# K and V transposed on PE as 4-byte pairs in a one-token attention kernel with its backward pass

## The chip, the cores and the metric

The kernel runs on one core of one Trainium2 chip. The metric is the device time of one execution in microseconds (us), as a median over several executions. Before the change it is 417.73 us (417.38 to 418.01, 4 runs). Ratios in this text are computed as the mean time of one kernel's fast runs over the mean time of the other kernel's fast runs of the same rounds, so they are not quite the ratio of the medians quoted beside them.

PE is the matrix engine (PEld its weight loads), DVE the vector engine, ACT the scalar engine, POOL and SP the two engines that here mostly issue transfers. A "DMA engine" is one of the 16 that move the core's data.

## The reference

One query token attends to a cache of 4096 keys and values in 32 heads of 128, in bf16; a small MLP is mixed in by a sigmoid gate. The kernel must return the output and the gradients of nine inputs, among them those of the whole K and V cache.

```python
q = (x @ wq)                                   # x: 1x640, wq: 640x4096 -> 32 heads of 128
s = einsum("bhqd,bhkd->bhqk", q, k_cache) * 128 ** -0.5
p = softmax(s)
o = einsum("bhqk,bhkd->bhqd", p, v_cache)
out = g * (o @ wo) + (1 - g) * mlp(x)          # g = sigmoid(sum(x * gate_w))
# and the vector-Jacobian product of out with grad_out for all inputs but B_x
# ... k_cache, v_cache and their gradients: 32 x 4096 x 128 bf16, 33.5 MB each
```

The four large tensors are 134 of the 165 MB that are moved.

## The kernel before

A K or V tile holds one head: 128 partitions, and on each partition 32 rows of 128 bf16 numbers (J = 32 blocks, 8 KB per partition). The products with the query (for K) and with the incoming gradient (for V) contract over the 128 numbers of a row, so each block is transposed on PE first, copied from PSUM to SBUF by ACT, and used as the stationary operand of a small matmul:

```python
def transposes(src, c):                       # chunk c of 4: eight blocks
    tp = tr_ps.tile([P, 8, P], BF16, name="tr", tag="tr")
    for t in range(8):
        nc.tensor.transpose(tp[:, t, :], src[:, c * 8 + t, :], ident_bf[:])
    sb = tsb.tile([P, 8, P], BF16, name="tT", tag="tT")
    nc.scalar.copy(f32v(sb[...]), f32v(tp[...]))          # shapes cut
    return sb

def products(out, tb, c, vec):
    for t in range(8):
        j = c * 8 + t
        nc.tensor.matmul(out[:, j:j + W], lhsT=tb[:, t, :], rhs=vec.to_broadcast([P, W]), start=True, stop=True)
```

Two more sums run over the same tiles without a transpose:

```python
def o_part(a, b):                              # o = sum over j of V_j^T e_j
    for j in range(a, b):
        nc.tensor.matmul(O, lhsT=vts[h][:, j, :], rhs=st["e"][:, j:j + 1].to_broadcast([P, W]), ...)
...
for j in range(J):                             # dq
    nc.tensor.matmul(DQ, lhsT=kts[h][:, j, :], rhs=ds[:, j, 0:1].to_broadcast([P, W]), ...)
```

The loads of K and V are issued by SP three heads ahead, into four buffers each. The gradients dK and dV are outer products on DVE, stored by POOL:

```python
def load_k(h):
    kts[h] = kv_in.tile([P, J, Dh], BF16, name="Kn", tag="Kn", bufs=KB)
    nc.sync.dma_start(kts[h][:], Kv[h])
...
nc.gpsimd.dma_start(dVv[h], st["dV"][:])
```

Every matmul here is two PE instructions, a weight load and the matmul. The program is fully unrolled: 13,864 of these on PE alone.

## Time and profile before

| what | value | view |
|---|---|---|
| time | 417.73 us (span of the profiled run 415.7) | runs |
| traffic | 165.06 MB, 397 GB/s over the span | queue table |
| DMA share from 5 to 374 us | 1.01 at 415 GB/s | busy time by stretch |
| PE, DVE busy from 5 to 374 us | 295 and 284 of 369 us | busy time by stretch |
| PE instructions | 6,932 weight loads, 6,932 matmuls | page, part 1 |

The first lines are the busy time by stretch of the kernel before: for each stretch the busy us and the number of instructions of the five engines, the clock granted to PE, the mean busy share of the 16 DMA engines, and what they moved.

```profile
core 0: us, PE busy (x) PEld busy (x) DVE busy (x) ACT busy (x) POOL busy (x), PEclk, DMA share, GB/s
5.00:374.00 369.00, 295.24 (x6715) 272.23 (x6716) 284.36 (x740) 168.88 (x382) 41.17 (x73) 0.95 1.01 415
374.00:403.00 29.00, 10.40 (x217) 8.90 (x216) 22.99 (x60) 4.21 (x11) 7.32 (x11) 0.69 0.95 379
403.00:416.00 13.00, 0.00 (x0) 0.00 (x0) 0.00 (x0) 0.00 (x0) 0.00 (x0) 0.50 0.06 23
```

To the eye the DMA is full until 403 us. Here is the same view of the last microseconds in 5 us steps:

```profile
395.00:400.00 5.00, 0.45 (x1) 0.18 (x1) 4.75 (x20) 0.00 (x0) 1.45 (x2) 0.50 1.01 394
400.00:405.00 5.00, 0.27 (x1) 0.09 (x1) 0.88 (x5) 0.25 (x1) 0.00 (x0) 0.50 0.66 251
405.00:410.00 5.00, 0.00 (x0) 0.00 (x0) 0.00 (x0) 0.00 (x0) 0.00 (x0) 0.50 0.06 26
```

From 405 to 410 us no engine computes and the DMA share is 0.06, one sixteenth, at 26 GB/s. One DMA engine is at work; the other 15 have finished.

The queue table of the page (queue, kind: packets, MB, share of the 16 engines' time) lists the loads (q1), the stores (q0) and the fetching of instructions (q8, q14):

```profile
q1 hardware_dynamic: 14116, 82.03, 48.6%
q0 software_dynamic: 12112, 82.03, 47.7%
q8 instruction: 54, 0.88, 0.8%
q14 instruction: 14, 0.11, 0.1%
```

These are the groups of instructions that the change touches (line, engine, operation, out<-in, shapes, count | busy us, mean ns of one | idle before and what ended it). L537 is the PSUM copy, L535 the transposes, L543 the products, L385 the only matmuls whose weights are read with a stride (36 bytes):

```profile
L537 ACT COPY tT<-tr 128x512 f32<-128x512 f32 x256 | 142.9, 587 | 153.1 <-PE tr L535 153.0
L543 PEld LDWEIGHTS <-tT 128*128 128x128 bf16 x2048 | 75.8, 98 | 37.0 <-ACT tT L537 31.6
L535 PE MATMUL tr<-ident_bf,Kn 128*128 128x128 bf16 x1024 | 79.2, 230 | 9.4 <-DMA Kn<-in_A_k_cache_dram 8.2
...
L535 PEld LDWEIGHTS <-Kn 128*128 128x128 bf16 x1024 | 66.2, 104 | 10.9 <-DMA Kn<-in_A_k_cache_dram 9.3
...
L543 PE MATMUL sA<-qdc,tT 128*128 128x48 bf16 x1024 | 49.2, 188 | 23.0 <-ACT dq_all L659 16.3
...
L385 PEld LDWEIGHTS <-w_sb 128*96 128x96 bf16 x90 | 17.6, 272 | 1.6 <-issue 0.6
```

Last, three lines of PE's timeline (start us, duration us, engine, line, operation). Eight bf16 transposes take 0.61 us, of which the last is 0.22, so they start 56 ns apart; the fp32 transpose of L609 occupies PE for 0.11 us before the next one starts:

```profile
201.13 1.05 PE L535 MATMUL tr<-ident_bf,Vn 128*128 128x128 bf16 x16
202.03 0.28 PE L609 MATMUL sA<-ident_f,m 128*128 128x128 f32 x1
202.14 0.61 PE L535 MATMUL tr<-ident_bf,Vn 128*128 128x128 bf16 x8
```

### The profile page before, as it was taken

The numbers are of one execution on the slowest core, as the hardware profiler recorded it, in microseconds if no ns is written. First come the engines' busy times: TensorE is split into PE (matmuls) and PEld (weight loads), VectorE is DVE, ScalarE is ACT, GpSimd is POOL, SyncE is SP. The second block draws the span as 40 slices with busy tenths as digits, with TensorE's granted clock in tenths as the row PEclk, the third lists the DMA queues.
The fourth block names the chain that finished last, engine by engine and source line by source line (L and its number), as shares of the span: only waits on it lengthen the run. The fifth ranks groups of instructions, "written<-read, shape, count | busy, mean of one in ns | idle before, by whom it ended". The sixth has DMA issues, their size and how long they took to land.

```text
span 415.7 us, 15639 instructions
## 1 busy us (share of the span) xinstructions
PE 305.6 (74%) x6932; PEld 281.1 (68%) x6932; DVE 308.2 (74%) x804; ACT 174.4 (42%) x394; POOL 49.3 (12%) x92
## 2 busy tenths in 40 slices
PE   0787999888998788788877688429888788876200
PEld 0676888888987677787767687428777678876200
DVE  2348666665679999989897688528999997967850
ACT  1354444334445455354533346305553545553000
POOL 0001110111110111121111112001111111132310
PEclk9999999969999999989996899958999999998655
DMA  8999999999999999999999999999999999998980
GB/s 280 419 401 335 420 424 417 420 423 423 421 423 420 420 404 415 424 420 423 423 410 426 423 414 411 419 422 381 405 411 423 419 419 422 421 422 351 401 314 14
DMA packets 26336, 165.06 MB, mean 397 GB/s; under 512 B 2812, under 2 KB 2812, under 8 KB 10012
## 3 DMA queue, kind: packets, MB, share of 16 engines
q1 hardware_dynamic: 14116, 82.03, 48.6%
q0 software_dynamic: 12112, 82.03, 47.7%
q8 instruction: 54, 0.88, 0.8%
q14 instruction: 14, 0.11, 0.1%
q10 hardware_dynamic: 40, 0.01, 0.0%
HBM read 82.03 MB, written 82.03 MB: 395 GB/s over the span
## 4 chain that ended last, share of the span: by engine, by line
DMA 37%; DVE 30%; PE 21%; ACT 6%; issue 2%; ACTq 0%; DVEq 0%
DMA Kn<-in_A_k_cache_dram 30%; PE tr L535 7%; DVE dK_sb L557 7%; DVE dV_sb L557 6%; DMA out_dram<-dK_sb 6%; ACT tT L537 5%; DVE junk L354 4%; PE sA L601 3%; PE sA L543 3%; PE sB L654 3%; DVE junk L268 3%; PE h_ps L385 2%; DVE junk L486 2%; DMA vec_rows<-in_gate_w_dram 1%; DVE wo_g L343 1%
## 5 line engine op out<-in xcount | busy, mean ns | idle before, releaser
L537 ACT COPY tT<-tr 128x512 f32<-128x512 f32 x256 | 142.9, 587 | 153.1 <-PE tr L535 153.0
L543 PEld LDWEIGHTS <-tT 128*128 128x128 bf16 x2048 | 75.8, 98 | 37.0 <-ACT tT L537 31.6
L535 PE MATMUL tr<-ident_bf,Kn 128*128 128x128 bf16 x1024 | 79.2, 230 | 9.4 <-DMA Kn<-in_A_k_cache_dram 8.2
L557 DVE TENSOR_TENSOR dV_sb<-p_bf,qd 128x2048 bf16<-128x2048 bf16 x64 | 78.0, 1218 | 4.1 <-DMA out_dram<-dK_sb 4.1
L557 DVE TENSOR_TENSOR dK_sb<-ds_bf,qd 128x2048 bf16<-128x2048 bf16 x64 | 77.7, 1216 | 0.0
L535 PEld LDWEIGHTS <-Kn 128*128 128x128 bf16 x1024 | 66.2, 104 | 10.9 <-DMA Kn<-in_A_k_cache_dram 9.3
L535 PE MATMUL tr<-ident_bf,Vn 128*128 128x128 bf16 x1024 | 72.8, 221 | 0.2 <-DMA Vn<-in_A_v_cache_dram 0.2
L543 PE MATMUL sA<-qdc,tT 128*128 128x48 bf16 x1024 | 49.2, 188 | 23.0 <-ACT dq_all L659 16.3
L535 PEld LDWEIGHTS <-Vn 128*128 128x128 bf16 x1024 | 63.2, 100 | 1.4 <-issue 0.7
L543 PE MATMUL sB<-qdc,tT 128*128 128x48 bf16 x1024 | 46.3, 183 | 0.6 <-issue 0.6
L654 PE MATMUL sB<-ds_bf,Kn 128*128 128x48 bf16 x1024 | 32.6, 185 | 7.7 <-DVE ds_bf L643 4.8
L584 POOL DMA_DIRECT2D out_dram<-dV_sb x32 | 18.3, 571 | 169.1 <-DVE dV_sb L557 82.1
L601 PEld LDWEIGHTS <-Vn 128*128 128x128 bf16 x1024 | 30.3, 96 | 10.4 <-issue 10.3
L601 PE MATMUL sA<-e_bf,Vn 128*128 128x48 bf16 x1024 | 30.9, 183 | 7.4 <-DVE zs L621 5.4
L574 POOL DMA_DIRECT2D out_dram<-dK_sb x31 | 17.7, 570 | 153.1 <-DVE rz L623 84.6
L654 PEld LDWEIGHTS <-Kn 128*128 128x128 bf16 x1024 | 29.7, 97 | 8.3 <-issue 8.3
L605 DVE TENSOR_REDUCE m<-sA 128x1 f32<-128x32 f32 x32 | 6.1, 189 | 31.7 <-PE sA L543 31.5
L268 DVE SCALAR_TENSOR_TENSOR junk<-wo_g,da_bc 128x640 bf16<-128x640 bf16 x32 | 26.3, 821 | 2.9 <-DMA wo_g<-in_A_wo_dram 1.2
L354 DVE SCALAR_TENSOR_TENSOR junk<-wq_g,dq_bc 128x1024 bf16<-128x1024 bf16 (+1 forms) x25 | 25.1, 1004 | 0.2
L385 PE MATMUL h_ps<-cols_bf,w_sb 128*96 128x1 bf16 x90 | 18.3, 314 | 1.2 <-ACT qd L279 0.5
L641 DVE TENSOR_SCALAR_CACHE_REDUCE dj<-sB,rz 128x128 f32<-128x128 f32 x32 | 11.1, 345 | 10.8 <-PE sB L635 10.8
L385 PEld LDWEIGHTS <-w_sb 128*96 128x96 bf16 x90 | 17.6, 272 | 1.6 <-issue 0.6
(137 smaller groups left out, 277.5 us busy)
## 6 DMA issues: line engine op xcount, KB each, us to landing
Kn<-in_A_k_cache_dram SPq DMA_DIRECT2D x32, 1024.0 KB, 27.0
Vn<-in_A_v_cache_dram SPq DMA_DIRECT2D x32, 1024.0 KB, 27.8
out_dram<-dV_sb POOLq DMA_DIRECT2D x32, 1024.0 KB, 12.3
out_dram<-dK_sb POOLq DMA_DIRECT2D x31, 1024.0 KB, 12.4
wq_g<-in_A_wq_dram SPq DMA_DIRECT2D x4, 1280.0 KB, 21.8
wo_g<-in_A_wo_dram SPq DMA_DIRECT2D x8, 640.0 KB, 13.3
out_dram<-wo_g POOLq DMA_DIRECT2D x8, 640.0 KB, 11.3
out_dram<-dwq_t POOLq DMA_DIRECT2D x5, 896.0 KB, 16.2
```

What stands on the lines that cost most here:

```text
L268: nc.vector.scalar_tensor_tensor(junk[:, 0:D], in0=wos[g][:, i, :], scalar=1.0, in1=da_bc[:], op0=ALU.mult, op1=ALU.mult, accum_out=gp["do ...
L354: nc.vector.scalar_tensor_tensor(junk[:, c0:c1], in0=wqs[w][:, rc, c0:c1], scalar=1.0, in1=dq_bc[:, w * WG * Dh + c0:w * WG * Dh + c1], op ...
L385: nc.tensor.matmul(hps[a][:, fc:fc + 1], lhsT=w1_sb[:, rc, :].rearrange("p (q c) -> p q c", c=FCN)[:, :, fc], rhs=x_bf[:, rc:rc + 1], star ...
L535: nc.tensor.transpose(tp[:, t, :], src[:, c * 8 + t, :], ident_bf[:])
L537: nc.scalar.copy(f32v(sb[:].rearrange("p a b -> p (a b)")), f32v(tp[:].rearrange("p a b -> p (a b)")))
L543: nc.tensor.matmul(out[:, j:j + W], lhsT=tb[:, t, :], rhs=vec.to_broadcast([P, W]), start=True, stop=True)
L557: nc.vector.tensor_tensor(dst[:, a:b, :].rearrange("p j (a b) -> p j a b", b=2), col[:, a:b, :].unsqueeze(2).to_broadcast([P, n, Dh // 2, 2]),
L574: nc.gpsimd.dma_start(dKv[h], st["dK"][:])
L584: nc.gpsimd.dma_start(dVv[h], st["dV"][:])
L601: nc.tensor.matmul(O, lhsT=vts[h][:, j, :], rhs=st["e"][:, j:j + 1].to_broadcast([P, W]), start=(j == 0), stop=(j == J - 1))
L641: nc.vector.tensor_scalar(dj[:], PT, rz[:], None, ALU.mult, ALU.add, accum_out=dd[:])
L654: nc.tensor.matmul(DQ, lhsT=kts[h][:, j, :], rhs=ds[:, j, 0:1].to_broadcast([P, W]), start=(j == 0), stop=(j == J - 1))
```

## The change

Two neighbouring bf16 numbers are moved through the transpose as one 4-byte number. One transpose then handles two blocks: 16 per K or V tile, 32 per head, in place of 64. After it, partition p holds a pair of numbers (2p', 2p'+1) of the even block (p < 64) or the odd block. The query is therefore laid out as two columns per half of the pair, zero in the other block's partitions ("block-diagonal"), and two accumulating matmuls, one per half of the pair, give the products of both blocks. The number of products stays at 64 per head. The intent was to halve the transposes.

```diff
     def transposes(src, c):
-        tp = tr_ps.tile([P, 8, P], BF16, name="tr", tag="tr")
-        for t in range(8):
-            nc.tensor.transpose(tp[:, t, :], src[:, c * 8 + t, :], ident_bf[:])
-        sb = tsb.tile([P, 8, P], BF16, name="tT", tag="tT")
...
+        tp = tr_ps.tile([P, 4, P], F32, name="tr", tag="tr")
+        flat = f32v(src[:].rearrange("p j d -> p (j d)"))
+        for t in range(4):
+            k = c * 4 + t
+            nc.tensor.transpose(tp[:, t, :], flat[:, k * P:(k + 1) * P], ident_f[:])
+        sb = tsb.tile([P, 4, P], F32, name="tT", tag="tT")
+        nc.scalar.copy(sb[...], tp[...])
+        return sb[...].bitcast(BF16).rearrange("p (a b two) -> p a two b", a=4, two=2)
 
     def products(out, tb, c, vec):
-        for t in range(8):
-            j = c * 8 + t
-            nc.tensor.matmul(out[:, j:j + W], lhsT=tb[:, t, :], rhs=vec.to_broadcast([P, W]), start=True, stop=True)
+        for t in range(4):
+            k = c * 4 + t
+            for par in range(2):
+                nc.tensor.matmul(out[:, 2 * k:2 * k + W], lhsT=tb[:, t, par, :],
+                                 rhs=vec[:, par, :].unsqueeze(1).to_broadcast([P, W // 2, 2]),
+                                 start=(par == 0), stop=(par == 1))
# cut: the masks mask2 and sel2, three zeroed tiles for the columns, and per group of four heads
# two small DVE products, one matmul and two ACT copies that build the block-diagonal columns,
# in place of two small DVE products
```

## The prediction

> What bounds the kernel now: the DMA. In the table of busy time by stretch, the DMA engines' share is 1.01 from 5 to 374 us at 415 GB/s, with PE busy 295 of those 369 us and DVE 284. From 374 to 403 us it is still 0.95 (one hole, 0.71 from 375 to 380). The 165.06 MB (queue table) at the 420 GB/s of the good slices alone take about 393 us of the 415.7 us span. The Trainium skill ("DMA: Bandwidth & Descriptors", "Where 436 GB/s comes from") gives 435 GB/s as the fabric's ceiling; these slices are near it. The change moves no data byte. K loads wait for buffers that PE frees, but stores keep the DMA full meanwhile.
>
> What the change does, per head (K and V):
> - Transposes: 64 bf16 become 32 fp32. In the timeline eight bf16 transposes take 0.61 us, the last one 0.22: 56 ns start to start. The fp32 transposes already in the kernel (lines 609, 635) last 292 and 319 ns against about 220, and the next transpose follows line 609's after 0.11 us (202.03 to 202.14). So I take 111 ns, two bf16 transposes: 64 x 56 = 3.58 us become 32 x 111 = 3.55 us. Nothing is saved. The skill ("TensorE: Matmul & The Clock Gate", "Weight-path perf modes") says fast weight load has no win for fp32; the fp32 loads here do take 138 to 164 ns against 98, but I expect them hidden behind the matmuls.
> - PSUM copies on ACT: the same 8, 128x512 fp32, 587 ns.
> - Products: the same 64 matmuls of 48 columns (25 ns start to start), but their weights are read with a step of 2 elements. The only strided weights here (line 385, step 18) load in 272 ns instead of 98, 179 ns apart. I expect step 2 to be nearly free; at worst about 60 ns (estimate: 179 ns for 96 columns is 1.9 ns each, every one on a new 16-byte line; here 32 lines). That adds 64 x 35 ns = 2.2 us.
> - Preparation, 8 groups: two small DVE operations stay two; a matmul and two short ACT operations are added, about 0.8 us of latency.
> - 2,048 fewer PE instructions: the instruction queue's 0.88 MB falls by some 0.13 MB, 0.3 us of DMA.
>
> How much is on the critical path: almost nothing. The chain of waits shows PE transposes at 7%, between DMA waits (37%), and their sum doesn't change. A head takes 11.6 us on average and 9.1 us where it catches up, so even 2 us more on PE would mostly be hidden. The tail after 374 us is stores, DVE (23 of 29 us) and the last landings.
>
> Predicted: 417.4 us, 415 to 422 in 8 of 10. Faster by over 2%: 0.02; within 2%: 0.90; slower by over 2%: 0.08.
>
> What would show it: DMA share about 1.0 from 5 to 374 us; 1,024 transposes at about 111 ns spacing, PE busy within 10% of 305.6 us; ACT copies 256 x 587 ns; DVE unchanged; product weight loads below 150 ns.
>
> What would make it wrong: fp32 transposes at 220 ns (weight load not hidden, or four passes), adding 3.5 us per head, or slow strided loads: PE would near 100% and the DMA share fall below 0.95, giving 425 to 460 us. A gain over 2% would need the 12 us after 403 us to vanish.

## More of the kernel before

The 54 packets of q8 are 16 KB each. 54 x 256 instructions of 64 bytes is about what PE's 13,864 instructions need, so q8 is PE's instruction queue. The Trainium skill ("Runtime: NRT & Kernel Launch", section "Instruction fetch mechanics") says that an engine's sequencer fetches its own instructions by DMA in 16 KiB blocks of 256; this trace agrees.

## The result, and the profile after

The changed kernel is correct and takes 414.09 us (413.68 to 414.78, 4 runs): ratio 0.9915, 95% interval 0.9898 to 0.9932. That is inside the class "within 2%", but 0.9 us below the predicted range, and the gain of 3.6 us is ten times the 0.3 us that the prediction found a reason for. Executions over 1.5% slower than the fastest of the same kernel are left out of the means.

Almost everything in the profile is as before. The same groups after the change (the lines are now L561, L559, L568):

```profile
L561 ACT COPY tT<-tr 128x512 f32<-128x512 f32 x256 | 142.3, 587 | 140.9 <-PE tr L559 140.2
L568 PEld LDWEIGHTS <-tT 128*128 128x128 bf16 x2048 | 80.4, 98 | 40.3 <-ACT tT L561 34.9
L559 PE MATMUL tr<-ident_f,Kn 128*128 128x128 f32 x512 | 80.7, 295 | 6.5 <-DMA Kn<-in_A_k_cache_dram 6.5
...
L568 PE MATMUL sA<-qd,tT 128*128 128x48 bf16 x1024 | 48.8, 187 | 23.5 <-ACT dq_all L686 12.8
L559 PEld LDWEIGHTS tr<-ident_f,Kn 128*128 128x128 f32 x512 | 60.1, 150 | 7.6 <-issue 6.2
```

Half the transposes, 80.7 us in place of 79.2 for K; the copies take the same 587 ns; the products' weight loads, now with a step of two elements, the same 98 ns. PE is busy 305.7 us (305.6 before), DVE 308.8 (308.2). The timeline gives the reason, again three lines:

```profile
199.11 1.07 PE L559 MATMUL tr<-ident_f,Vn 128*128 128x128 f32 x8
200.02 0.27 PE L636 MATMUL sA<-ident_f,m 128*128 128x128 f32 x1
200.13 0.60 PE L559 MATMUL tr<-ident_f,Vn 128*128 128x128 f32 x4
```

Eight fp32 transposes take about as long as sixteen bf16 ones. In the whole trace their median distance is 109 ns, against 56 ns.

The stretch from 5 to 374 us is the same to 1 GB/s, and the end comes earlier, but looks alike: one engine at 26 GB/s.

```profile
5.00:374.00 369.00, 296.94 (x5740) 270.27 (x5741) 286.83 (x745) 171.71 (x398) 41.21 (x73) 0.96 1.01 416
```

```profile
395.00:400.00 5.00, 0.28 (x1) 0.09 (x1) 1.25 (x5) 0.25 (x1) 0.00 (x0) 0.50 0.86 348
400.00:405.00 5.00, 0.00 (x0) 0.00 (x0) 0.00 (x0) 0.00 (x0) 0.00 (x0) 0.50 0.06 26
405.00:410.00 5.00, 0.00 (x0) 0.00 (x0) 0.00 (x0) 0.00 (x0) 0.00 (x0) 0.50 0.03 12
```

What did change is in the queue table:

```profile
q1 hardware_dynamic: 14116, 82.03, 48.8%
q0 software_dynamic: 12112, 82.03, 47.8%
q8 instruction: 46, 0.75, 0.7%
q14 instruction: 14, 0.11, 0.1%
```

Eight blocks of PE instructions fewer: 54 became 46, as PE's instructions fell by 2,032.

### One DMA engine is behind the others

A transfer over 128 partitions runs on all 16 DMA engines, and the trace has the time at which each of the 16 reported its share landed (as increments of the transfer's semaphore, without the engine's name). The list is worked out from these events, for one of the load queue's semaphores and for the last two large stores: time of the first of the 16 landings, then how much later the 15th and the 16th came.

```
                 before                          after
          first   15th    16th          first   15th    16th   (us)
loads       6.6   +0.8    +0.8            6.1   +0.9    +0.9
           46.6   +3.0    +3.8           45.7   +2.4    +4.5
          114.0   +7.5    +8.1          114.1   +6.5    +6.7
          190.7   +9.2   +14.9          189.8   +8.1   +13.7
          227.8   +9.1   +16.4          226.6   +9.7   +15.1
          307.1   +4.3   +16.3          304.6   +5.4   +15.9
          347.1   +3.1   +16.6          344.7   +4.4   +15.4
stores    398.4   +1.4    +8.7          394.3   +1.8    +9.2
          399.7   +1.3    +8.6          395.6   +1.8    +9.2
```

At the start all 16 are together. From about 190 us on, one engine alone lands 5 to 14 us behind the 15th, and the span ends when it has done its last share. Once it is some 15 us behind, the distance stops growing. A load counts only when all 16 have landed and the buffers hold few heads, so I take it that the other engines are then held to the pace of the slow one; this is argued from the list, not measured.

### The profile page after: what moved, and what is told of

It reads as the page before. It is cut to its first block, busy times and chain, and to the rows that moved or that the text cites. A ratio compares the mean times of both kernels' runs of the same rounds, so it can differ in the third digit from the quotient of the medians.

```text
span 412.1 us, 13687 instructions
## 1 busy us (share of the span) xinstructions
PE 305.7 (74%) x5916; PEld 277.5 (67%) x5916; DVE 308.8 (75%) x807; ACT 177.0 (43%) x410; POOL 49.9 (12%) x95
## 4 chain that ended last, share of the span: by engine, by line
DVE 33%; PE 30%; DMA 23%; ACT 7%; issue 3%; ACTq 0%; DVEq 0%
DMA Kn<-in_A_k_cache_dram 17%; PE tr L559 10%; DVE dK_sb L584 8%; DVE dV_sb L584 7%; DMA out_dram<-dK_sb 6%; ACT tT L561 6%; PE sA L628 4%; DVE junk L376 4%; PE sA L568 3%; PE h_ps L407 3%; PE sB L681 3%; DVE junk L279 2%; DVE junk L508 2%; PE sB L568 1%; DMA vec_rows<-in_gate_w_dram 1%
## 5 line engine op out<-in xcount | busy, mean ns | idle before, releaser
L561 ACT COPY tT<-tr 128x512 f32<-128x512 f32 x256 | 142.3, 587 | 140.9 <-PE tr L559 140.2
L568 PEld LDWEIGHTS <-tT 128*128 128x128 bf16 x2048 | 80.4, 98 | 40.3 <-ACT tT L561 34.9
L559 PE MATMUL tr<-ident_f,Kn 128*128 128x128 f32 x512 | 80.7, 295 | 6.5 <-DMA Kn<-in_A_k_cache_dram 6.5
L559 PE MATMUL tr<-ident_f,Vn 128*128 128x128 f32 x512 | 72.6, 277 | 0.1
L568 PE MATMUL sA<-qd,tT 128*128 128x48 bf16 x1024 | 48.8, 187 | 23.5 <-ACT dq_all L686 12.8
L559 PEld LDWEIGHTS tr<-ident_f,Kn 128*128 128x128 f32 x512 | 60.1, 150 | 7.6 <-issue 6.2
L559 PEld LDWEIGHTS tr<-ident_f,Vn 128*128 128x128 f32 x512 | 56.8, 143 | 0.2 <-PE sA L568 0.2
L568 PE MATMUL sB<-qd,tT 128*128 128x48 bf16 x1024 | 46.1, 183 | 0.1
L628 PEld LDWEIGHTS <-Vn 128*128 128x128 bf16 x1024 | 30.2, 96 | 10.4 <-issue 10.4
L681 PEld LDWEIGHTS <-Kn 128*128 128x128 bf16 x1024 | 29.2, 97 | 3.8 <-issue 3.8
```

Source lines behind the costliest of these rows:

```text
L559: nc.tensor.transpose(tp[:, t, :], flat[:, k * P:(k + 1) * P], ident_f[:])
L561: nc.scalar.copy(sb[:].rearrange("p a b -> p (a b)"), tp[:].rearrange("p a b -> p (a b)"))
L568: nc.tensor.matmul(out[:, 2 * k:2 * k + W], lhsT=tb[:, t, par, :], rhs=vec[:, par, :].unsqueeze(1).to_broadcast([P, W // 2, 2]), start=(pa ...
```

## The theory and its rivals

- F (fetch): PE's instruction blocks all come through one DMA engine. This engine must also carry its sixteenth of the data, so it ends last. Eight blocks fewer end the kernel earlier by about 3.6 us, 0.45 us a block.
- P: what counts is the time that PE takes, or when it frees buffers.
- S: one DMA engine is slow for another reason, and the gain came from elsewhere (the hole at 375 us, the start). For such a reason the Trainium skill ("DMA: Bandwidth & Descriptors", section "Latency and other measured facts") has a candidate: it calls DMA engines 7 and 15 usually slower and names, as its best guess, the descriptor rings of transfers that POOL issues, as it does the stores here.
- T: the 4-byte transposes are better for the DMA in themselves.

F is the theory as it stood when the expectations were written. Its first clause, one engine for all blocks, does not hold in the traces (see "Which DMA engine it is").

## The experiments

Eighteen kernels ran. Except d1, each was timed in five rounds against the kernel before.

### The number of instructions, and the time of PE

e1_more_instr and e2_more_time add work to the changed kernel that nothing reads:

```diff
 # e1_more_instr, after the dq sum of each head
+        for _ in range(32):
+            nc.tensor.matmul(B[:, 511:512], lhsT=ident_bf[:], rhs=ident_bf[:, 0:1], start=True, stop=True)
 # e2_more_time, at the same place
+        for _ in range(8):
+            nc.tensor.transpose(B[:, 384:512], ident_f[:], ident_f[:])
```

> The kernel after the change, plus 32 tiny matmuls (one column, 25 ns apart) per head: 2,048 more PE instructions, about 0.8 us more PE time per head. Theory F (all of PE's instruction blocks come through one DMA engine, which ends last; 3.6 us for 8 blocks, 0.45 us a block): 54 blocks again and 417 to 418.5 us. Rival P (the gain came from the time PE takes): the same change as in e2_more_time, whatever it is. Rival S (one DMA engine is slow for another reason and the gain came from elsewhere, e.g. the hole at 375 us): 414 us.

> The kernel after the change, plus 8 fp32 transposes (111 ns apart) per head: about 0.9 us more PE time per head, as much as e1_more_instr, but only 512 more instructions, 2 blocks. Theory F: 48 blocks, 414.6 to 415.4 us, some 2.7 us faster than e1_more_instr. Rival P: the same time as e1_more_instr. Rival S: 414 us.

Measured: e1_more_instr 424.66 us, ratio 1.0151 (1.0109 to 1.0192), 54 blocks; e2_more_time 416.86 us, ratio 0.9983 (0.9965 to 1.0002), 48 blocks. Both missed. e1 is slower than e2, which P did not expect, but it is by 7 us, where F had 2.7; and e2 is slower than F allowed. The busy time of one stretch shows why these runs are not clean. The same 30 us of the changed kernel, of e1_more_instr and of e2_more_time:

```profile
125.00:155.00 30.00, 24.74 (x533) 22.39 (x531) 28.99 (x81) 15.58 (x38) 3.19 (x6) 1.00 1.01 419
```

```profile
125.00:155.00 30.00, 26.49 (x552) 24.65 (x548) 26.08 (x66) 13.59 (x32) 2.90 (x7) 0.89 0.95 363
```

```profile
125.00:155.00 30.00, 26.24 (x525) 24.26 (x524) 29.18 (x79) 15.77 (x39) 3.20 (x6) 1.00 0.98 383
```

The DMA fell from 419 to 363 and 383 GB/s. The likely reason, which no run tests, is that with 0.8 us more per head PE, which is busiest while the MLP's strided matmuls run (up to 121 us in the kernel before), made the DMA wait. So adding instructions is a poor test. Why e1 lost that much more than e2 stays open; its granted clock in this stretch was also lower (0.89 against 1.00), and its traced run (420.07 us) is the fastest of its six.

Taking instructions away has no such problem. e3_fewer_instr and e4_before_fewer leave out every second matmul of the two sums (wrong result), in the kernel after and in the kernel before:

```diff
-            for j in range(a, b):
+            for j in range(a, b, 2):
...
-        for j in range(J):
+        for j in range(0, J, 2):      # stop flags moved to the last matmul that is left
```

> The kernel after the change with every second matmul of the two accumulations over 32 blocks left out (wrong result on purpose): 2,048 fewer PE instructions and 0.8 us less PE time per head. Theory F: 38 blocks, 410 to 411 us. Rival S: 414 us. Rival P: faster too, so this run alone doesn't part F from P; e2_more_time does.

> The kernel before the change, with the same matmuls left out (wrong result on purpose): the 2-byte transposes stay, but PE has 2,048 fewer instructions, 46 blocks as after the change. Theory F: 413.5 to 414.8 us, all of the change's gain without the change. Rival S, and a rival T by which the gain comes from the 4-byte transposes themselves: 417.7 us.

Measured: e4_before_fewer 414.24 us, ratio 0.9921 (0.9902 to 0.9940). The kernel with the old bf16 transposes and as many PE instructions as the changed one has the changed one's time. T falls, and so does what S says of the gain, that it came from elsewhere. Its line of the queue table:

```profile
q8 instruction: 46, 0.75, 0.7%
```

e3_fewer_instr, 38 blocks, has 412.07 us, ratio 0.9875 (0.9853 to 0.9896): faster than after the change, but by 1.7 us where F had 3.6.

Both runs also shorten PE's time. e7_fewest_same_time leaves out 30 of 32 matmuls of each sum and puts 7 fp32 transposes in their place, so that PE works as long with fewer instructions; e6_fewest leaves them out only.

```diff
-            for j in range(a, b):
+            for j in range(a, b, 16):
...
+        for _ in range(7):                      # e7 only, after each of the two sums
+            nc.tensor.transpose(B[:, 384:512], ident_f[:], ident_f[:])
```

> The kernel after the change with 30 of 32 matmuls of each of the two accumulations left out (wrong result on purpose) and 7 fp32 transposes put in for each (7 x 111 = 0.77 us for 30 x 25 = 0.75 us): PE's time stays, its instructions fall by 2,944, some 11 blocks, to 34 or 35 blocks. Theory F (PE's instruction blocks load one DMA engine that ends last), at 0.3 to 0.45 us a block: ratio to before 0.978 to 0.985, about 408 to 411 us. Rival P (PE's time is what counts): 0.9915, 414 us, as after the change.

> The same without the transposes put in: 3,840 fewer PE instructions than after the change, 15 blocks fewer, 31 blocks, and 1.5 us less PE time per head (wrong result on purpose). Theory F: 3 or 4 blocks less than e7_fewest_same_time, so 1 to 1.5 us faster, 407 to 410 us. Rival P: well below e7_fewest_same_time, by several us.

Measured: e7_fewest_same_time 410.28 us, ratio 0.9813 (0.9791 to 0.9835), 35 blocks; e6_fewest 409.47 us, ratio 0.9800 (0.9780 to 0.9820), 31 blocks. The stretch and the queue line of e7_fewest_same_time:

```profile
5.00:374.00 369.00, 301.59 (x4354) 274.68 (x4355) 289.48 (x749) 172.43 (x401) 43.19 (x76) 0.96 1.01 418
```

```profile
q8 instruction: 35, 0.57, 0.5%
```

PE is busy 302 us, 5 more than after the change (297), and the kernel is 4 us faster. Then e6 takes 32 us of PE's busy time away (269 us in the same stretch) and gains only another 0.8 us, no more than its four blocks explain and less than the two intervals can tell apart. So P falls as the reason of the gain: it is the number of PE instructions, not PE's time.

| kernel | blocks of 16 KB | ratio to before | us per block saved |
|---|---|---|---|
| before | 54 | 1 | |
| after (three times, with e5 and e16 below) | 46 | 0.9915, 0.9907, 0.9917 | 0.43 to 0.49 |
| e4_before_fewer | 46 | 0.9921 | 0.41 |
| e3_fewer_instr | 38 | 0.9875 | 0.33 |
| e7_fewest_same_time | 35 | 0.9813 | 0.41 |
| e6_fewest | 31 | 0.9800 | 0.36 |

(The last column is 417.7 us times the gain, over the blocks saved.)

e5_sp_nops was to tell PE's instruction fetch from that of another engine:

```diff
+        for _ in range(64):
+            nc.sync.nop()
```

> The kernel after the change plus 64 no-ops per head on the SP engine, 2,048 instructions, 128 KB more to be fetched, but not by PE. Theory F in its narrow form (PE's queue has its own DMA engine, and only that one ends late): 414 us, as after the change, with more packets in the other instruction queue. If any instruction fetch costs alike: 417 us.

Measured: 414.35 us, ratio 0.9907 (0.9889 to 0.9924). This says nothing about the question: the trace has the same 13,687 instructions as after the change, so the no-ops were dropped when the program was built. It counts as a repeat of the changed kernel. What other engines' fetching costs is left open.

### Which DMA engine it is

The Trainium skill ("DMA: Bandwidth & Descriptors", section "Why a DMA increments its semaphore by 16 and not by 1") says that a transfer is split over the largest number k of engines, up to 16, that divides the size of its slowest dimension (the first that is longer than 1) on both sides, and that a transfer issued by SP runs on the k lowest-numbered ones. d1_which_engine makes use of it:

```diff
+        if h == 26:
+            scr = const.tile([16, 16, 16], BF16, name="scr")
+            for k in range(1, 17):
+                nc.sync.dma_start(scr[0:k, k - 1, :], A_wo[0:k, 0:16])
```

> The kernel after the change with 16 tiny loads issued right behind the loads of head 29: load k has k rows, 1 to 16. By the Trainium skill a load of k rows runs on the k lowest-numbered DMA engines. Theory F: one engine is 10 to 16 us behind on this queue. Tiny loads that use it land that much later than those that don't, so the smallest late k names the engine. If no engine is the slow one: all 16 tiny loads land within 2 us or so.

Measured (one look, correct, 414.97 us), from the landing events of these transfers:

```
load just before, 128 rows: 15 landings 333.4 to 337.8, the 16th at 348.9 us
rows   issued    landings (us)
  1    323.6     333.9
  2    324.8     333.9  334.3
  3    325.8     333.8  334.2  334.9
  4    329.2     334.2  334.9  335.2  335.4
  5    333.9     336.9  337.0  337.0  338.2  349.7
  6    338.5     339.7  339.7  339.8  340.2  341.2  350.3
  7    343.7     344.9  344.9  344.9  344.9  344.9  344.9  350.7
  8    348.9     353.7 ... 354.1
```

With up to four rows none is late; with five, six and seven rows exactly one is, right behind the late landing of the load before. So the rule of k holds here, and the slow engine is the 5th. (From the 8th on the tiny loads were issued when it had caught up.) Does it also bring PE's instructions? That was assumed in the runs below, and the traces speak against it.

The following was worked out from the start and end of every DMA packet in the 20 traces; no view of the profile shows it. On one DMA engine the next packet starts 3 to 4 ns before the last one ends (so it is in the tail after 403 us, where only one engine works). Packets can therefore be joined into chains, one per engine, as far as the fit is unique.

- While a block of PE's instructions is in flight (1.0 us on average in the kernel before), 15.2 data packets are in flight on average in place of 16.2. So a block does take one DMA engine's time.
- It is not always the same engine. In 373 cases a block's chain could be followed past the next block: that was never on the same chain.
- The late engine's chain could be followed past 63 blocks, and none of them was on it. As a check of the method, 265 of 279 pairs of late landings that should share a chain did, and chains begun at random held 4.4% of the blocks that they passed, where 16 engines taken evenly would give 6%.
- What the late engine's chain shows instead are slow data packets. From 190 to 375 us 13% of its 8 KB packets that could be followed (104 to 158 in each of these traces) take 30 to 80 ns longer than the usual 309 ns in the kernel before, 15% after the change and 8% in e6_fewest; on the other engines it is 0.7, 0.4 and 0.3%.

So the 5th engine is late, and fewer PE instructions end the kernel earlier, but not because their blocks pass through that engine. By what way the number of instructions reaches it stays open. One rival that no run excludes is the recording of the profile, which grows with the number of instructions: every timed run lists a clock and a span, and none is without.

### More or less data on the 5th engine

e8, e9 and e10 issue ten of the 32 K loads as five transfers each, cut so that the 5th engine gets fewer, more, or as many rows as before:

```diff
-            nc.sync.dma_start(kts[h][:], Kv[h])
+            cuts = (0, 112, 116, 120, 124, 128) if h % 3 == 0 and h else (0, P)   # e8_less_on_5th
+            # e9_more_on_5th: (0, 112, 117, 122, 127, 128);  e10_even_split: (0, 64, 80, 96, 112, 128)
+            for a, b in zip(cuts, cuts[1:]):
+                nc.sync.dma_start(kts[h][a:b], Kv[h][a:b])
```

> The kernel after the change; ten of the 32 K loads are each issued as five transfers, of 112, 4, 4, 4 and 4 rows. The run with tiny loads named the 5th DMA engine as the slow one. Here the four small pieces run on the first four engines, so the 5th gets 7 rows of 8 KB instead of 8 per such load, 0.31 us less, and the first four get 11. Theory F: 3 us faster than e10_even_split, 411 to 412 us if the extra transfers cost nothing. Rivals (no particular engine ends last): the same time as e10_even_split and e9_more_on_5th.

> The same, with pieces of 112, 5, 5, 5 and 1 rows: now the 5th engine gets 10 rows per such load, 0.62 us more than in the kernel after the change, and the first one 11 as in e8_less_on_5th. Theory F: 5 to 7 us slower than e10_even_split and 8 to 10 us slower than e8_less_on_5th, about 420 us. Rivals: the same time as those two.

> The control: the same ten loads as five transfers of 64, 16, 16, 16 and 16 rows, 8 rows for every DMA engine as before. All theories: 414 us plus what five transfers cost instead of one, which I expect to be under 2 us.

Measured: e8 427.49 us (ratio 1.0220), e9 435.03 us (1.0429), e10 426.39 us (1.0195). More rows on the 5th cost 9.8 us against the control (by the ratios), more than the 5 to 7 expected; fewer rows gained nothing, where F had 3 us. The control itself cost 12 us, not 2: in its trace new K loads waited for earlier K loads 25 times, 57 us in all (twice and 6 us after the change), probably because more transfers per load share the load queue's eight semaphores. So only half of this can be read.

e11, e12 and e13 touch two loads only, and nearly the same cut reverses the roles:

```diff
+            m = 116 if h in (8, 18) else P      # e11; e12: 115; e13: 64
+            for a, b in ((0, m), (m, P)):
+                if a < b:
+                    nc.sync.dma_start(kts[h][a:b], Kv[h][a:b])
```

> The kernel after the change; the K loads of heads 8 and 18 are each cut into 116 and 12 rows. By the rule that the tiny loads followed, 116 rows run on 4 engines, 29 rows each, and 12 rows on 12 engines, one each: the first four get 30 rows instead of 8, the 5th gets 1, the last four none. Theory F (the 5th DMA engine, which also brings PE's instructions, ends last): 14 rows of 8 KB less for it, 4.3 us; 410 to 413 us, as the first four may now end as late. Rival (no special engine; the one with most rows ends last): slower than e12_cut_115.

> The same cut one row earlier: 115 rows run on 5 engines, 23 each, and 13 rows on 13 engines, one each. The first four get 24 rows, 6 fewer than in e11_cut_116, but the 5th gets 24 as well. Theory F: 32 rows more for the 5th engine than after the change, 9.9 us: 421 to 425 us, about 12 us slower than e11_cut_116. Rival: faster than e11_cut_116.

> The control: the two loads cut in half, 8 rows for every engine as before. All theories: 414 us, within 1 us of the kernel after the change.

Measured: e11_cut_116 420.45 us (1.0059, 1.0039 to 1.0078), e12_cut_115 427.04 us (1.0218, 1.0196 to 1.0241), e13_cut_64 415.14 us (0.9939, 0.9918 to 0.9959). e12 is 6.6 us slower than e11, although its most loaded engines have 6 rows fewer per load; the order is F's and not the rival's. It needs only that the 5th engine is the late one, whatever makes it late. But e11 is 5 us slower than the control, where F had it faster. Its last large store points to the cause: four engines land 3.8 to 7.8 us late, where after the change it is one. Presumably the four that took over 22 rows per load had become late themselves; the landings carry no names.

e14 and e15 tried to give those four more room, by smaller or later cuts; e16 is the changed kernel again.

```diff
+            m = 68 if h in (17, 21, 25) else P      # e14_late_cuts: K loads, cut as above
+            m = 116 if g in (4, 5, 6) else P        # e15_wo_cuts: wo loads, cut the same way
```

> The kernel after the change; the K loads of heads 17, 21 and 25 are cut into 68 rows (4 engines, 17 each) and 60 rows (15 engines, 4 each): the first four engines get 21 rows instead of 8, the 5th gets 4, the last none. Theory F: 12 rows, 3.7 us, less for the 5th engine; 1 to 4 us faster than e16_after_again. Rival (no special engine): not faster, rather slower.

> The kernel after the change; the wo loads of groups 4, 5 and 6, which are needed late, are cut into 116 and 12 rows of 5 KB: the 5th engine gets 21 rows, 4.0 us (0.19 us a row), less, the first four 66 rows, 12.7 us, more. Theory F: 1 to 4 us faster than e16_after_again, unless the first four then end last. Rival: not faster.

> The kernel after the change, unchanged: ratio 0.99 to before, about 414 us.

Measured: e14 420.96 us (1.0072), e15 419.14 us (1.0034), e16 414.13 us (0.9917, 0.9897 to 0.9937). Both trials are slower than the changed kernel, by 6.5 and 4.9 us. From 250 to 350 us they fall about 7 us behind it in bytes moved (386 and 388 GB/s against 415). The likely reason is that a load is there only when its last engine has landed, so that a load on four engines is slow for everything queued behind it; this was not tested. F's expectation for these two was wrong: being behind on one engine does not make delays on others free.

The last run cuts a store, which nothing waits for, at the end, when 15 engines are known to have 7 us left:

```diff
     def dwq_store(rc):
+        if rc == 0:
+            for a, b in ((0, 92), (92, P)):
+                nc.sync.dma_start(dwq_v[a:b, rc, 0:CL], dwqt[rc][a:b, 0:CL])
+            return
         nc.gpsimd.dma_start(dwq_v[:, rc, 0:CL], dwqt[rc][:, 0:CL])
```

> The kernel after the change; one of the five stores of dwq near the end (128 rows of 7 KB, 0.27 us a row on one DMA engine) goes out through the SP queue in two pieces, of 92 rows (4 engines, 23 each) and 36 rows (12 engines, 3 each). The 5th engine writes 3 rows instead of 8, 1.35 us less; the first four write 26, 4.9 us more, inside the 7 us by which they finish earlier. Theory F: 1 to 2 us faster than after the change, ratio 0.987 to 0.989 to before, and a shorter stretch at the end with one engine at 26 GB/s. Rival (no special engine): 0.9915 or slower.

Measured: correct, 412.76 us (411.72 to 413.15), ratio 0.9867 (0.9838 to 0.9895). The changed kernel in the run before this one had 0.9917 (0.9897 to 0.9937), so the intervals just part (that of the repeat e5, 0.9889 to 0.9924, overlaps). All six times lie below all 16 of the changed kernel, the lowest of which is 413.42 us; the gain over the change is about 2 us. The end now looks like this:

```profile
395.00:400.00 5.00, 0.45 (x1) 0.18 (x1) 4.72 (x18) 0.00 (x0) 0.86 (x1) 0.50 1.01 415
400.00:405.00 5.00, 0.27 (x1) 0.09 (x1) 0.19 (x2) 0.26 (x1) 0.00 (x0) 0.50 0.46 187
405.00:410.00 5.00, 0.00 (x0) 0.00 (x0) 0.00 (x0) 0.00 (x0) 0.00 (x0) 0.50 0.02 8
```

From 400 to 405 us the DMA moves 187 GB/s where it was 26, and the 16th landing of the last large store comes 5.2 us after the first instead of 9.2 us. Part of the first figure is a shift: in this trace the last large stores begin to land 3 us later. Taking 5 rows, 1.35 us, from the 5th engine did what a late 5th engine predicts; it does not tell why that engine is late. An even cut of this store through the SP queue was not run, so the change of queue is not ruled out as the reason. It is also the fastest correct version.

## Why the prediction was right or wrong

- "Transposes: 32 x 111 = 3.55 us, nothing is saved": right. The median distance is 109 ns, PE's busy time 305.7 against 305.6 us, and the fp32 weight loads (150 ns) stay hidden.
- "PSUM copies the same 8", "DVE unchanged": right, 587 ns each, 308.8 against 308.2 us.
- "I expect step 2 to be nearly free": right, 98 ns a load and 25 ns between matmuls; the bad case of 2.2 us per head did not come.
- "DMA share about 1.0 from 5 to 374 us": right, 1.01 at 416 GB/s, and it was the trap. The share is a mean over 16 engines and says nothing about which of them ends last.
- "the instruction queue's 0.88 MB falls by some 0.13 MB, 0.3 us of DMA": the bytes are right (0.75 MB are left), and this is the step that failed. The term was sized by its bytes at the speed of all 16 engines. It measures 3.5 us (0.9917, e16), or 0.33 to 0.49 us per block of 16 KB over the runs. e4 and e7 show that this term is all of the gain: the old transposes with as many instructions have the same time, and fewer instructions at the same PE time gain more. The effect was named and its size was wrong by a factor of ten. What the bytes do not account for is that the end hangs on one late engine, which loses more time the more instructions PE has; by what way stays open.
- "A gain over 2% would need the 12 us after 403 us to vanish": these 12 us were called "the last landings" and not looked at. In 5 us steps, 7 of them are one DMA engine at 26 GB/s. Reading that line before predicting would have led to the late engine, though not to its tie with PE's instructions.
- "even 2 us more on PE would mostly be hidden": not tested at 2 us. In e2, 0.9 us more per head, 28 us in all, made the kernel 2.8 us slower, of which two blocks explain under 1 us: mostly hidden, but not free. The change did not need this slack.

An estimate shows how close the tie is: an 8 KB packet takes 0.309 us in the trace, a sixteenth of the 164 MB of data 387 us. Begun at 2 us, that leaves 22 us of the 411 us until the late engine's last packet in the kernel before, 18.5 us of 407.5 after the change and 13 us of 402 in e6_fewest: 0.41, 0.40 and 0.43 us for each of the 54, 46 and 31 blocks, if the engine never idled. In seven other traces (e1 to e5, e7, e16) the same sum gives 0.40 to 0.46 us. As the chains show, it is time lost on its data packets or between them, in proportion to the number of PE instructions.

## What to carry to other kernels

When the DMA bounds a kernel, look at which of the 16 DMA engines ends last: a stretch at the end with a share of 1/16, or a 16th landing well after the 15th, means that a mean share of 1.0 hides one late engine. In this unrolled kernel with many small matmuls, each 256 PE instructions cost 0.33 to 0.49 us at the end, so a change that saves PE no time can still save time by saving instructions. To unload the late engine, cut transfers that nothing waits for (e17); cutting loads made the kernel slower. And a sum that closes is no proof of its mechanism: here it closed for a path that the traces contradict.

## What the Trainium skill lacked or had wrong

- "Runtime: NRT & Kernel Launch", "Instruction fetch mechanics", describes the 16 KiB blocks and calls their cost mostly hidden. It does not say what they can cost when the DMA is full, nor how they are dealt to the DMA engines. Here 19 blocks fewer at about the same PE time made the kernel 1.9% faster (e7_fewest_same_time), 0.41 us a block, and the next block was on another engine in all 373 cases that could be followed.
- "DMA: Bandwidth & Descriptors", "Latency and other measured facts", names DMA engines 7 and 15 as the usually slow ones. In this kernel one engine was slow, the 5th (d1_which_engine), some 15 us behind on the loads and 9 us on the last stores.
- The same page, "Why a DMA increments its semaphore by 16 and not by 1": its rule for k and the lowest-numbered engines held for loads of 2 to 7 rows. It gives no cost in time of an uneven cut: two loads cut so that four or five engines carry most rows made the kernel 5 and 12 us slower than an even cut.
- "TensorE: Matmul & The Clock Gate" has no figure for a stream of fp32 transposes. Here they start 109 ns apart, against 56 ns for bf16, with weight loads of 143 to 150 ns hidden behind them; a step of two elements in the weights cost nothing (98 ns).
